# Halved GpSimd instructions, spread weight pieces and opening loads by head, in a fused masked attention and expert layer

## The chip, the cores and the metric

One core of a Trainium2 chip. The metric is the device time of one execution in microseconds (us). Engines: TensorE (PE; PEld is its weight load), VectorE (DVE), ScalarE (ACT), GpSimd (POOL) and SyncE (SP), which issues the DMAs.

## What is computed

```
# q, k, v: (8, 8, 576, 64) f32;  tau = 0.02
scores = q @ k^T / 8
scores = where(scores >= max(scores) - tau, scores, -1e9)      # per row
attn   = exp(scores - max);  attn = attn / (sum(attn) + 1e-9)
x      = (attn @ v), heads joined                              # 4608 x 512
h      = x @ w_in                                              # w_in 512 x 2048, float64
g      = max(h, 0) + alpha * min(h, 0)
out    = g @ w_out                                             # w_out 2048 x 512, float64; out f32
```

## The kernel before

The attention works on 32 pairs of heads, each cut into nine units (a block of 128 query rows of one head, and one unit for the rests of both). The main loop (L832) runs over cycles, one unit each, from cycle -3 to the 288 units and 9 more. In a cycle each engine gets the steps of several units at different depths: scores on TensorE (L403, two cycles ahead, into one of two PSUM buffers), the row maximum on VectorE (L418), the exponential and the threshold on ScalarE (L426, L431), the mask and row sum on VectorE (L438, for the cycle's own unit), transposes (L447), their copies out (L499 to L507), products with v (L550), and for a pair that has ended the reciprocal, the scaling and the store to DRAM (L566 to L604; L597 and L603 are GpSimd's). Up to unit 52 the row maxima go two by two in odd cycles.

Most products are computed with operands split into a rounded part and a rest (two fp32r numbers). For the keys and queries of the pairs after the first, ScalarE rounds (L336, L353) and GpSimd makes the rest (L340, L365); SP moves halves to the other partitions. Pair 0 is prepared in `prep_first` with the rests on VectorE (L327, L330). The pairs 0 to 3 are "whole": their attention weights and v are not split.

The expert layer starts when x of a batch of four pairs is there (`RDY`, cycle 49 for the first). Its first weights are 14 pieces (seven of w_in, seven of w_out, `F1`), float64 words which class `Split64` turns into two fp32r numbers. A piece has a load (SP, L115) and steps that `decode_at` puts into cycles after its start c: at c two ScalarE instructions (L125, L126), at c+1 to c+4 one VectorE instruction each (L129, L132, L137, L142), at c+4 ScalarE's rounding (L146), at c+5 two GpSimd instructions (L150, L151), at c+6 GpSimd's join (L154). The starts are -3, 0, 3, ... 15 for the input pieces and 16, 19, ... 34 for the output pieces. Raw words lie in the slot of a later weight; those of the last output piece in one of two buffers that the loads of k, q and v of the pairs use too. The temporaries come from a pool of four (`spool`, closed at cycle 41) and, after it, from the 11 places (`GB`) of the expert layer's `g` tiles.

Order is written out by hand: instructions stand on each engine in the order in which the cycles emit them, and each engine works its queue in that order. The planner `Mlp` fits first-layer and second-layer products of the expert layer into a cycle by a budget of TensorE time (`room`), and holds back the first layer while 11 `g` tiles live. After the last pair the rest of the expert layer runs alone.

The opening (L819 to L831): SP issues four loads of pair 0's keys, four of its queries, tau, the first weight piece, pair 1's keys and queries, alpha; VectorE's first instruction is tau's negative (L824), then come the splits of `prep_first`.

Of the kernel before, what the change touches and what calls it, by code (L numbers as in the profile page):

```python
# [52 lines left out]
XO = 1  # L53
L2O = 3
# [6 lines left out]
DEC0, DEC = -3, 3  # L61
DECO0, DECO = 16, 3
# [4 lines left out]
def f(ap):  # L67
    return ap.bitcast(F32)


@with_exitstack
def tile_masked_attention_moe(
# [31 lines left out]
    class Split64:  # L104


        def __init__(self, pool, raw, temp_pool, temp, eng, src, a, name):
# [9 lines left out]
        def size(self):  # L117
# [4 lines left out]
            if pool is mem:  # L122
                pool, tag, bufs = (mem.mp1, "g", GB) if mem.mp1 else (spool, "wt", 4)
            self.t = pool.tile([P, DM], I32, tag=tag, name=f"wt{self.name}", bufs=bufs)
            nc.scalar.activation(f(self.t), f(self.high), AF.Abs)  # L125
            nc.scalar.activation(f(self.low), self.low.bitcast(U32), AF.Copy, scale=2.0**-52)  # L126

# [15 lines left out]

        def round(self, hi):
            self.hi = hi
            nc.scalar.activation(hi, f(self.t), AF.Copy)  # L146

        def rest(self):
            low, t = f(self.low), f(self.t)
            self.eng[1].tensor_tensor(low, low, f(self.high), op=ALU.mult)  # L150
            self.eng[2].tensor_tensor(t, t, f(self.hi), op=ALU.subtract)  # L151

        def join(self, lo):
            nc.gpsimd.tensor_tensor(lo, f(self.t), f(self.low), op=ALU.add)  # L154
# [86 lines left out]
    mem = SimpleNamespace(mp1=None)  # L241
# [33 lines left out]
    class Pair:  # L275
# [9 lines left out]
        def load(self, what):  # L285
# [11 lines left out]
            if pi == 0:  # L297

                r = ap1.tile([P, KW if what == "k" else 2 * S], F32, tag="vst" if what == "k" else "p", name=f"{what}r{pi}", bufs=2)
                for j in range(2):  # L300
                    n = w if j else S
                    for half in range(2):
                        nc.sync.dma_start(r[half * D : (half + 1) * D, j * S : j * S + n], src[j * D : (j + 1) * D, :n])
                if what == "k":
                    self.kr = r
                else:
                    self.qr = r[:, : 2 * S].rearrange("p (a b) -> p a b", a=2)
# [8 lines left out]
            else:  # L316
                self.qr = r

# [19 lines left out]
        def prep_kl(self):  # L338
            self.kl = ap1.tile([P, KW], F32R, tag="kl", name=f"kl{self.pi}", bufs=2)
            nc.gpsimd.tensor_tensor(self.kl[:, S:], self.kr, f(self.kh[:, S:]), op=ALU.subtract)  # L340
# [19 lines left out]
        def prep_ql(self):  # L360
            self.qt = ap1.tile([P, S], F32R, tag="qt", name=f"qt{self.pi}", bufs=1)
            if QLV and self.pi >= QLV:
                nc.vector.scalar_tensor_tensor(self.qt, self.qr, 0.125, f(self.qst[:, 0, :S]), op0=ALU.mult, op1=ALU.subtract)
                return
# [674 lines left out]
```

## Time and profile before

| | us |
|---|---|
| median of three runs | 1379.86 |
| the runs | 1378.5 to 1380.6 |
| the profiled execution's own time | 1380.41 |
| its span, first to last instruction | 1378.6 |

In the profile, busy times are the time in which an engine had an instruction, waits inside the instruction included; PE stands for matmuls, whose ends are modelled. L12 is line 12 of the kernel before. The granted TensorE clock is given as a share of full speed.

### The profile page before, as it was taken

How to read it: one execution, taken by the hardware profiler on the slowest of the kernel's cores; microseconds unless marked ns; L12 is line 12 of the kernel's file. 1: busy time of each engine (PE TensorE's matmuls, PEld its weight loads, DVE VectorE, ACT ScalarE, POOL GpSimd, SP SyncE). 2: the span in 40 equal slices, each digit the busy share in tenths (PEclk: the TensorE clock that was granted, in tenths of full speed). 3: DMA queues.
4: the chain of work that ended last, by engine and by line, in shares of the span. 5: the costliest groups of instructions: out<-in, count | busy, mean ns of one | idle time of the engine just before them, and what ended most of it. 6: DMA issues, size and time to landing. Idle time of an engine off the chain costs nothing.

```text
span 1378.6 us, 23959 instructions
## 1 busy us (share of the span) xinstructions
PE 1332.7 (97%) x8116; PEld 1180.2 (86%) x8116; DVE 994.5 (72%) x1970; ACT 842.5 (61%) x1915; POOL 814.9 (59%) x891
## 2 busy tenths in 40 slices
PE   5888899999999999999999999999999999999998
PEld 4556789999999999999999998898888888888887
DVE  6999888888888888889888883883655644333332
ACT  6878888888888888888888873542323321211210
POOL 3776566666666575766666654884757554443431
PEclk9999999999999999999999999999999999999999
DMA  8644643644643644445445413345455452343222
GB/s 252 173 138 112 164 110 109 175 124 112 172 135 114 167 126 128 141 133 142 132 129 150 120 55 110 117 144 169 156 181 187 134 184 92 102 152 113 92 77 77
DMA packets 115178, 186.05 MB, mean 135 GB/s; under 512 B 18320, under 2 KB 49328, under 8 KB 115056
## 3 DMA queue, kind: packets, MB, share of 16 engines
q1 hardware_dynamic: 115056, 184.52, 45.2%
q8 instruction: 65, 1.06, 0.3%
q14 instruction: 57, 0.47, 0.1%
HBM read 104.41 MB, written 37.90 MB: 103 GB/s over the span
## 4 chain that ended last, share of the span: by engine, by line
PE 85%; DVE 6%; ACT 4%; issue 1%; DMA 1%; POOL 1%; SPq 0%; POOLq 0%; DVEq 0%; ACTq 0%
PE accj L232 19%; PE phj L196 18%; PE av L550 11%; PE s L403 11%; PE acca L232 9%; PE pha L196 9%; PE t L447 7%; DVE p L438 2%; DVE nmx L418 1%; PE tk L463 1%; DMA wri<-in_moe_w_in_dram 1%; ACT xb L563 1%; ACT xa L561 1%; ACT xh L182 1%; ACT p L426 0%
## 5 line engine op out<-in xcount | busy, mean ns | idle before, releaser
L418 DVE TENSOR_REDUCE nmx<-s 128x1 f32<-128x576 f32 x288 | 217.2, 754 | 73.2 <-PE s L403 70.1
L223 ACT ACTIVATE gj<-ptj 128x512 fp32r<-128x512 f32 (+1 forms) x109 | 62.9, 577 | 338.1 <-DVE ptj L215 338.1
L226 POOL TENSOR_TENSOR gj<-ptj,gj 128x512 fp32r<-128x512 f32 (+1 forms) x109 | 129.2, 1186 | 237.2 <-ACT gj L223 236.5
L232 PE MATMUL accj<-wo,gj 128*128 128x512 f32 x1140 | 262.4, 390 | 0.6 <-POOL gj L226 0.6
L232 PEld LDWEIGHTS accj<-wo,gj 128*128 128x128 f32 x1140 | 213.9, 188 | 45.1 <-POOL gj L226 1.0
L196 PE MATMUL phj<-xhj,wi 128*128 128x512 f32 (+1 forms) x816 | 232.8, 367 | 0.0
L438 DVE SCALAR_TENSOR_TENSOR p<-s,thr,p 128x576 f32<-128x576 f32 x256 | 206.8, 808 | 1.6 <-ACT thr L431 1.2
L426 ACT ACTIVATE p<-s,nmx 128x576 f32<-128x576 f32 x256 | 190.1, 742 | 10.2 <-DVE nmx L418 9.9
L232 PE MATMUL acca<-wo,ga 128*128 128x512 f32 x588 | 186.1, 423 | 1.6 <-POOL ga L226 0.8
L403 PE MATMUL s<-kh,qst 128*128 128x288 f32 x640 | 142.5, 313 | 38.3 <-DVE p L438 22.1
L196 PEld LDWEIGHTS phj<-xhj,wi 128*128 128x128 f32 x816 | 147.6, 188 | 25.2
L214 DVE TENSOR_SCALAR ptj<-phj,alpha_sb 128x512 f32<-128x512 f32 (+1 forms) x109 | 74.2, 681 | 124.4 <-PE phj L196 120.4
L196 PE MATMUL pha<-xh,wi 128*128 128x256 f32 x784 | 156.9, 284 | 0.2 <-ACT pra L209 0.2
L447 PE MATMUL t<-ident,p 128*128 128x128 f32 x1024 | 154.8, 274 | 0.0
L403 PEld LDWEIGHTS s<-kh,qst 128*128 128x128 f32 x640 | 101.6, 193 | 61.2 <-issue 31.2
L196 PE MATMUL phj<-xlj,wi 128*128 128x512 f32 (+1 forms) x408 | 150.0, 368 | 1.1 <-POOL xlj L810 0.9
L962 DVE TENSOR_TENSOR obj<-accj,pinj 128x512 f32<-128x512 f32 x72 | 49.8, 692 | 138.5 <-PE accj L232 127.7
L403 PE MATMUL s<-kl,qst 128*128 128x288 f32 x640 | 133.7, 299 | 0.0
L196 PEld LDWEIGHTS pha<-xh,wi 128*128 128x128 f32 x784 | 128.1, 190 | 4.4 <-ACT pra L209 1.5
L447 PEld LDWEIGHTS t<-ident,p 128*128 128x128 f32 x1024 | 126.6, 141 | 0.1
L232 PEld LDWEIGHTS acca<-wo,ga 128*128 128x128 f32 x588 | 102.1, 192 | 13.7 <-POOL ga L226 1.2
L219 POOL TENSOR_TENSOR pta<-pta,pra 128x256 f32<-128x256 f32 x94 | 69.4, 739 | 73.9 <-ACT pra L209 71.3
(123 smaller groups left out, 2865.5 us busy)
## 6 DMA issues: line engine op xcount, KB each, us to landing
pinj<-part SPq DMA_DIRECT2D x72, 256.0 KB
kr<-in_k_dram SPq DMA_DIRECT2D x31, 320.0 KB
rb<-rvd SPq DMA_DIRECT2D x64, 144.0 KB
xs<-xa SPq DMA_DIRECT2D x32, 288.0 KB
part<-obj SPq DMA_DIRECT2D x36, 256.0 KB
out_dram<-obj SPq DMA_DIRECT2D x36, 256.0 KB
vr<-in_v_dram SPq DMA_DIRECT2D x28, 320.0 KB
qr<-in_q_dram SPq DMA_DIRECT2D x31, 288.0 KB
```

The costliest lines, as they stand in the source:

```text
L196: nc.tensor.matmul(ph[:, :n], w[:, c, :], xx[:, c, :n], start=(c == 0 and ti == 0), stop=(c == NCC - 1 and ti == 2),)
L214: nc.vector.tensor_scalar(t[:, :n], ph[:, :n], 0.0, alpha_sb[:, fc : fc + 1], op0=ALU.min, op1=ALU.mult)
L219: nc.gpsimd.tensor_tensor(t[:, :n], t[:, :n], r[:, :n], op=ALU.add)
L223: nc.scalar.activation(g[:, 0, :n], t[:, :n], AF.Copy)
L226: nc.gpsimd.tensor_tensor(g[:, 1, :n], t[:, :n], f(g[:, 0, :n]), op=ALU.subtract)
L232: nc.tensor.matmul(acc[:m, :], gg[:, g, o : o + m], w, start=(first and ti == 0), stop=(last and ti == 2))
L403: nc.tensor.matmul(ps[:, h, :288], w, kk[:, a + h * 288 : a + (h + 1) * 288], start=(ki == 0 and i == 0), stop=(ki == 1 and i == n - 1),)
L418: nc.vector.tensor_reduce(self.nmx[:, j : j + 1], self.S[u][0][:, :, :288], axis=AX.XY, op=ALU.max, negate=True)
L426: nc.scalar.activation(pj, ps[:, :, :288], AF.Exp, bias=nmx[:, j : j + 1], scale=1.0)
L438: nc.vector.scalar_tensor_tensor(pj, ps[:, :, :288], thr[:, j : j + 1], pj, op0=ALU.is_ge, op1=ALU.mult, accum_out=self.sm[:, c : c + 1])
L447: nc.tensor.transpose(tb[:, c, :], pt[:, j, j * D + c * P : j * D + (c + 1) * P], ident)
L550: nc.tensor.matmul(pa[:m, :n], w, x, start=(part == 0 and c == 0), stop=(part == z.parts[-1] and c == NKC))
```

## The change

Three things are done. GpSimd's two-tensor instructions of the 14 pieces, of the key and query rests of pairs 1 to 4, and of the scaling of pairs 0 to 3 are each issued as two instructions over half of the columns. The starts of the 14 pieces become -1, 2, 5, 9, 13, 17, 21 (input) and 25, 29, 34, 41, 44, 48, 52 (output); the pieces from cycle 41 on take their temporaries from the `g` places, so the count of living `g` tiles is replaced by a ring in which both stand in order. The loads of pair 0 are issued head by head (keys, then queries), and tau's negative stands behind the splits on VectorE.

```diff
+ROOM = GB - 1
-DEC0, DEC = -3, 3
-DECO0, DECO = 16, 3
+DECC = (-1, 2, 5, 9, 13, 17, 21, 25, 29, 34, 41, 44, 48, 52)
...
+def halves(eng, out, a, b, op):
+
+    h = out.shape[1] // 2
+    for c in (slice(0, h), slice(h, None)):
+        eng.tensor_tensor(out[:, c], a[:, c], b[:, c], op=op)
...
                 pool, tag, bufs = (mem.mp1, "g", GB) if mem.mp1 else (spool, "wt", 4)
+                self.place = None
+                if mem.mp1:
+                    self.place = [False]
+                    mem.ring.append(self.place)
...
+        def turns(self, eng, out, a, b, op):
+            if self.split:
+                halves(eng, out, a, b, op)
+            else:
+                eng.tensor_tensor(out, a, b, op=op)
...
         def rest(self):
             low, t = f(self.low), f(self.t)
-            self.eng[1].tensor_tensor(low, low, f(self.high), op=ALU.mult)
-            self.eng[2].tensor_tensor(t, t, f(self.hi), op=ALU.subtract)
+            self.turns(self.eng[1], low, low, f(self.high), ALU.mult)
+            self.turns(self.eng[2], t, t, f(self.hi), ALU.subtract)
 
         def join(self, lo):
-            nc.gpsimd.tensor_tensor(lo, f(self.t), f(self.low), op=ALU.add)
+            self.turns(nc.gpsimd, lo, f(self.t), f(self.low), ALU.add)
+            if self.place:
+                self.place[0] = True
...
+        def load_first(self):
+            self.kr = ap1.tile([P, KW], F32, tag="vst", name=f"kr{self.pi}", bufs=2)
+            qr = ap1.tile([P, 2 * S], F32, tag="p", name=f"qr{self.pi}", bufs=2)
+            self.qr = qr.rearrange("p (a b) -> p a b", a=2)
+            for j in range(2):
+                for r, src, w in ((self.kr, k, S + j * D), (qr, q, S)):
+                    for half in range(2):
+                        nc.sync.dma_start(
+                            r[half * D : (half + 1) * D, j * S : j * S + w], src[0, 0][j * D : (j + 1) * D, :w]
+                        )
...
         def prep_kl(self):
             self.kl = ap1.tile([P, KW], F32R, tag="kl", name=f"kl{self.pi}", bufs=2)
+            if self.pi <= WHOLE:
+                halves(nc.gpsimd, self.kl[:, S:], self.kr, f(self.kh[:, S:]), ALU.subtract)
+                return
...
+            if self.pi <= WHOLE:
+                halves(nc.gpsimd, self.qt, self.qr, f(self.qst[:, 0, :S]), ALU.subtract)
+                return
             nc.gpsimd.tensor_tensor(self.qt, self.qr, f(self.qst[:, 0, :S]), op=ALU.subtract)
...
         def fin_mul(self):
+            if self.whole:
+                halves(nc.gpsimd, self.x, self.x, self.rb, ALU.mult)
+                return
...
         def fin_out(self):
-            nc.gpsimd.tensor_tensor(self.x, self.x, self.rb, op=ALU.add)
+            if self.whole:
+                halves(nc.gpsimd, self.x, self.x, self.rb, ALU.add)
+            else:
+                nc.gpsimd.tensor_tensor(self.x, self.x, self.rb, op=ALU.add)
...
-            self.live += 1
+            st["place", fi] = [False]
+            mem.ring.append(st["place", fi])
...
             if o + P >= n:
-                self.live -= 1
+                st["place", fj][0] = True
...
-            if self.l1 and i >= self.gap and self.live < GB:
+            if self.l1 and i >= self.gap and all(p[0] for p in mem.ring[:-ROOM]):
...
-        c = DEC0 + DEC * n_ if n_ < F1 else DECO0 + DECO * (n_ - F1)
+        c = DECC[n_]
         load = max(-3, c - LD) if io == "i" else c - 3
...
         p.load("k")
-        p.load("q")
         nc.sync.dma_start(tau_sb, tau.partition_broadcast(P))
-        nc.vector.tensor_scalar(ntau_sb, tau_sb, -1.0, None, op0=ALU.mult)
         pieces[0][0].load()
...
         p.prep_first(0)
         p.prep_first(1)
+        nc.vector.tensor_scalar(ntau_sb, tau_sb, -1.0, None, op0=ALU.mult)
         p.load("v")
```

## Rows read from the trace of the kernel before

**Rows 1.** The page: its head, and PE's busy share in 40 equal slices of the span, in tenths.

```profile
span 1378.6 us, 23959 instructions
PE   5888899999999999999999999999999999999998
```

**Rows 2.** Busy time by stretch (us from the span's start): the stretch, its length, then for each engine busy us and number of instructions, granted clock, share of the DMA engines, GB/s. Pairs 0 to 3, pairs 4 to 6, pair 5 alone, and two pairs later on, each counted from the first row maximum of a pair to that of the next.

```profile
12.90:114.30 101.40, 86.21 (x454) 59.18 (x455) 96.49 (x176) 83.44 (x191) 66.91 (x56) 0.97 0.58 171
114.30:187.50 73.20, 63.53 (x435) 55.30 (x434) 66.80 (x146) 61.61 (x147) 45.82 (x50) 0.98 0.52 139
139.00:162.90 23.90, 18.09 (x129) 17.11 (x128) 20.96 (x46) 20.56 (x49) 11.44 (x11) 0.93 0.57 146
214.60:239.80 25.20, 25.20 (x184) 23.71 (x182) 21.98 (x49) 21.09 (x51) 14.60 (x19) 1.00 0.46 127
239.80:265.10 25.30, 25.30 (x179) 23.66 (x177) 21.81 (x49) 21.98 (x52) 15.18 (x17) 1.00 0.55 153
```

**Rows 3.** The same view for L418 alone, VectorE's row maximum, one for each unit: the stretch, its length, busy us and number. Pair 0 alone and pairs 0 to 3.

```profile
12.90:34.40 21.50, 6.76 (x9) 0.92 0.89 280
...
12.90:114.30 101.40, 27.04 (x36) 0.97 0.58 171
```

**Rows 4.** Groups of VectorE's instructions by line and shape, from 0 to 210 us, the four lines of the weight pieces (wti: input pieces, wto: output pieces): number, busy us, mean ns of one, idle time before them.

```profile
L137 DVE SCALAR_TENSOR_TENSOR wti<-wri,wti 128x512 int32<-128x512 int32 x7 | 8.5, 1221 | 0.0
L132 DVE TENSOR_SCALAR wto<-wto 128x512 int32<-128x512 int32 x7 | 8.4, 1197 | 0.0
L129 DVE TENSOR_SCALAR wto<-wto 128x512 f32<-128x512 f32 x7 | 7.2, 1035 | 0.0
...
L132 DVE TENSOR_SCALAR wti<-wti 128x512 int32<-128x512 int32 x7 | 5.0, 710 | 0.0
...
L137 DVE SCALAR_TENSOR_TENSOR wto<-wro,wto 128x512 int32<-128x512 int32 x7 | 4.9, 694 | 0.0
L142 DVE TENSOR_SCALAR wro<-wto 128x512 int32<-128x512 int32 x7 | 4.6, 652 | 0.0
...
L142 DVE TENSOR_SCALAR wri<-wti 128x512 int32<-128x512 int32 x7 | 3.4, 486 | 0.0
...
L129 DVE TENSOR_SCALAR wti<-wti 128x512 f32<-128x512 f32 x7 | 2.9, 419 | 0.0
```

**Rows 5.** The timeline around 23 us: start, us, engine, line, operation.

```profile
22.64 1.43 POOL L365 TENSOR_TENSOR qt<-qr,qst 128x576 fp32r<-128x576 f32 x1 [1.47 <-ACT qr L358]
...
22.77 1.84 DVE L137 SCALAR_TENSOR_TENSOR wti<-wri,wti 128x512 int32<-128x512 int32 x1
...
24.01 1.74 POOL L154 TENSOR_TENSOR wi<-wti,wri 128x512 fp32r<-128x512 f32 x1
```

**Rows 6.** Groups of GpSimd's instructions by line and shape over the whole span: number, busy us, mean ns of one, idle time before them and what ended it.

```profile
L226 POOL TENSOR_TENSOR gj<-ptj,gj 128x512 fp32r<-128x512 f32 x81 | 105.4, 1302 | 219.0 <-ACT gj L223 219.0
...
L226 POOL TENSOR_TENSOR ga<-pta,ga 128x256 fp32r<-128x256 f32 x98 | 72.3, 738 | 12.8 <-ACT ga L223 5.3
...
L154 POOL TENSOR_TENSOR wo<-wto,wro 128x512 fp32r<-128x512 f32 x16 | 22.8, 1428 | 1.5 <-DVE wto L151 1.2
L154 POOL TENSOR_TENSOR wi<-wti,wri 128x512 fp32r<-128x512 f32 x16 | 22.3, 1394 | 1.8 <-DVE wti L151 1.2
```

**Rows 7.** The timeline of the opening: start, us, engine, line, operation, idle time before it and what ended it. SPq rows are issues of DMAs, merged (x4).

```profile
0.74 2.48 SPq L303 DMA_DIRECT2D kr<-in_k_dram  x4
...
3.27 2.51 SPq L303 DMA_DIRECT2D qr<-in_q_dram  x4
4.44 0.68 ACT L326 ACTIVATE kh<-kr 128x576 fp32r<-128x576 f32 x1 [2.21 <-DMA kr<-in_k_dram]
...
6.99 0.68 ACT L329 ACTIVATE qst<-qr 128x576 fp32r<-128x576 f32 x1 [1.87 <-DMA qr<-in_q_dram]
...
8.21 0.68 ACT L329 ACTIVATE qst<-qr 128x576 fp32r<-128x576 f32 x1
...
8.90 5.74 SPq L115 DMA_DIRECT2D wri<-in_moe_w_in_dram  x5
9.30 0.15 DVE L824 TENSOR_SCALAR ntau_sb<-tau_sb 128x1 f32<-128x1 f32 x1 [9.30 <-DMA tau_sb<-in_tau_dram]
9.41 0.76 DVE L327 TENSOR_TENSOR kl<-kr,kh 128x576 fp32r<-128x576 f32 x1
...
11.01 0.85 PE L403 MATMUL s<-kh,qst 128*128 128x288 f32 x2 [11.01 <-DVE qst L330]
11.23 0.68 ACT L125 ACTIVATE wti<-wri 128x512 f32<-128x512 f32 x1 [2.34 <-DMA wri<-in_moe_w_in_dram]
...
12.97 0.75 DVE L418 TENSOR_REDUCE nmx<-s 128x1 f32<-128x576 f32 x1
...
14.81 0.74 ACT L426 ACTIVATE p<-s,nmx 128x576 f32<-128x576 f32 x1
```

**Rows 8.** Groups of ScalarE's instructions from 0 to 210 us, the three lines of a piece (one of each pair of groups): number, busy us, mean ns of one, idle time before them.

```profile
L126 ACT ACTIVATE wri<-wri 128x512 f32<-128x512 uint32 x7 | 4.7, 673 | 0.0
...
L125 ACT ACTIVATE wti<-wri 128x512 f32<-128x512 f32 x7 | 4.7, 670 | 2.3 <-DMA wri<-in_moe_w_in_dram 2.3
...
L146 ACT ACTIVATE wi<-wti 128x512 fp32r<-128x512 f32 x7 | 4.4, 622 | 0.0
```

More of the change, by code (lines that the diff above doesn't have):

```diff
@@ L104, in tile_masked_attention_moe, with __init__ @@
     class Split64:
-        def __init__(self, pool, raw, temp_pool, temp, eng, src, a, name):
+        def __init__(self, pool, raw, temp_pool, temp, eng, src, a, name, split=False):
+            self.split = split
             self.pool, self.raw_tag, self.temp_pool, self.temp_tag = pool, raw, temp_pool, temp
@@ L126, in size @@
             nc.scalar.activation(f(self.low), self.low.bitcast(U32), AF.Copy, scale=2.0**-52)
+        place = None
         def clamp(self):
@@ L240, in tile_masked_attention_moe @@
     spool = sp.enter_context(tc.tile_pool(name="spool", bufs=1, side="right"))
-    mem = SimpleNamespace(mp1=None)
+    mem = SimpleNamespace(mp1=None, ring=[])
     at, ps = ExitStack(), ExitStack()
@@ L297, in load @@
             if pi == 0:
[L299 to L307, printed above, removed]
+                self.load_first()
                 return
@@ L660, in __init__ @@
             self.acc = None
-            self.live = 0
             self.gap = 0
@@ L757, in tile_masked_attention_moe @@
     for fc in fcs1:
-        pieces.append((Split64(wp1, (f"wo{fc}", 1), mem, ("g", GB), ENG1[fc % 2], *src_i(fc)), fc, "i"))
+        pieces.append((Split64(wp1, (f"wo{fc}", 1), mem, ("g", GB), ENG1[fc % 2], *src_i(fc), split=True), fc, "i"))
     for fc in fcs1:
         stage = (wp1, (f"wo{fc + 1}", 1)) if fc + 1 < F1 else (ap1, ("raw", 2))
-        pieces.append((Split64(stage[0], stage[1], mem, ("g", GB), ENG1[fc % 2], *src_o(fc)), fc, "o"))
+        pieces.append((Split64(stage[0], stage[1], mem, ("g", GB), ENG1[fc % 2], *src_o(fc), split=True), fc, "o"))
     def decode_at(c, pool, w, fc, io, load):
```

## The prediction

> **What bounds the kernel now.** I read the page first, then busy times by stretch, then the timeline of the opening, then VectorE's groups. By the page [rows 1] TensorE is busy nearly everywhere except in the first slices, so what this change can win lies at the front. The stretches [rows 2] say where. In 239.8 to 265.1, an ordinary pair of the middle, PE is busy 25.30 of 25.30 us with 179 matmuls. In 12.9 to 114.3, the pairs 0 to 3 (36 row maxima [rows 3]), 454 matmuls take 101.4 us; VectorE is busy 96.49 us of it (95%), ScalarE 83.44 (82%), GpSimd 66.91 (66%). There VectorE sets the pace. In 114.3 to 187.5, the pairs 4 to 6, VectorE stands at 91%, and in pair 5 alone (139 to 162.9, no weight piece in it) at 88% beside ScalarE's 86%. Microseconds saved before about 200 us reach the end whole: what follows is TensorE's work, and its amount does not change.
>
> Much of VectorE's busy time is no work. Each weight piece takes four VectorE instructions, and the same instruction differs with what GpSimd does [rows 4]: L129 takes 419 ns on the input pieces and 1035 ns on the output pieces, L137 1221 and 694. One instance is plain [rows 5]: GpSimd's L365 starts at 22.64 and lasts 1.43 us, L137 starts at 22.77 and takes 1.84 us, so it did its 0.69 us of work only after L365, and GpSimd's next instruction, L154, takes 1.74 us instead of its mean 1.39 to 1.43 [rows 6], having waited in turn. The two engines exclude each other for an instruction at a time.
>
> **The change part by part.**
>
> *Price of a piece on VectorE.* The eight groups of [rows 4] sum to 44.9 us for 14 pieces. Unhindered, three instructions at 0.419 (L129's quick group, same shape) and one at 0.694 make 1.95 us a piece, 27.3 in all; the other 17.6 us are waiting, 1.26 us a piece.
>
> *Halves.* GpSimd's instructions for the pieces, for the key and query rests of pairs 1 to 4 and for the end of pairs 0 to 3 become two each. 256 columns take 738 ns and 512 take 1302 [rows 6]: a half is 0.57 of a whole, and a split costs 2 x 738 - 1302 = 174 ns. VectorE then waits out a half instead of a whole: 17.6 us become 17.6 x 0.57 = 10.0 us if collisions stay as frequent. GpSimd pays 58 x 0.174 = 10 us spread over some 160 us; at 66% busy it has that room. If the cover were gone, the price would be those 10 us.
>
> *Spreading.* By the code, before, 12.75 pieces have their VectorE steps in cycles up to 34, which is the stretch to 114.3; after, 9 (starts -1 to 29). So 3.75 pieces leave pairs 0 to 3 and fall to pairs 4 to 6 (starts 34 to 52). Pairs 0 to 3 lose on VectorE 3.75 x 1.95 = 7.3 us of work, and waiting falls from 12.75 x 1.26 = 16.1 to 9 x 1.26 x 0.57 = 6.5: 96.5 - 7.3 - 9.6 = 79.6 us. ScalarE loses 3.75 x (0.67 + 0.67 + 0.62) = 7.4 us [rows 8], leaving 76.0. At VectorE's present 95% the stretch would be 83.8 us; but ScalarE has nowhere in [rows 2] been above 87% (21.98 of 25.3), and at 87% it needs 87.4. I take 87.0, close to ScalarE's end: **-14.4 us**, bounds -9 (a share of only 86% of VectorE, below pair 5's) to -17.6.
>
> Pairs 4 to 6 gain VectorE work 7.3 us; their waiting goes from 1.25 x 1.26 = 1.6 to 5 x 1.26 x 0.7 = 4.4 us (0.7, not 0.57, since pairs from 5 on keep whole key and query rests and the ends of pairs 4 and 5 stay whole): 66.8 + 10.1 = 76.9. ScalarE has 61.6 + 7.4 = 69.0. At 95% VectorE needs 80.9, ScalarE at 87% needs 79.3. I take 80.2: **+7.0 us**, bounds +3.7 (no idle VectorE at all) and +10.
>
> *Opening.* Now the eight loads of pair 0 go keys first, then queries; each lands about 3 us after its issue: the last of the first head's queries is issued at 3.90 (second of four from 3.27) and ScalarE takes it at 6.99 [rows 7]. VectorE's first instruction is tau's negative, which waits for tau until 9.30; the key rest queued behind it had its input since 5.12. After: queries of head 0 take the third and fourth issue slots, 0.63 us apart, 2.00 and 2.63, and land near 5.8; L329 ends near 6.5, VectorE's key and query rests of head 0 near 7.3, the first scores start at 7.4 instead of 11.01. Head 1's queries land as before (8.21 for L329), so VectorE's last split ends near 9.7, then tau's negative (landed by 9.3: 0.15 us), and the first row maximum comes near 9.9 instead of 12.97. ScalarE then has the first exponential, the first piece (moved from cycle -3 to -1, its data there at 11.23) and the second exponential in a row, which gives some back. **-2.7 us**, bounds -1.9 (second exponential near 12.9 instead of 14.81) and -3.1.
>
> *At nothing.* Loads of later pieces move with their starts on SP's queue: three instead of five at cycle -3, which sends what follows earlier by up to 2 x 0.6 us; nothing waits for those loads, which come 8 to 12 cycles ahead for input pieces. The last output piece holds one of two raw buffers from cycle 49 to 58 instead of 31 to 40, so pair 7's queries, not pair 5's, get the late load: moved, not removed. The ring's new rule counts the four late pieces among 11 places; they are done by cycle 58, before the second group needs them. The pieces from cycle 41 on use the pool opened there, whose space pair 3 leaves at cycle 40: 0 to 2 us, taken as 0.
>
> *Sum*: -14.4 + 7.0 - 2.7 = -10.1 us. The profiled execution took 1380.4 (span 1378.6), 0.5 above the median 1379.9: I forecast **1370** for the median. A measurement here tells 0.2% (2.8 us) from no change.
>
> **The rivals.**
>
> *The waits don't shorten.* If GpSimd passes from half to half without letting VectorE in, waiting stays 1.26 us a piece. Pairs 0 to 3 then have 96.5 - 7.3 - 4.8 = 84.4, at 95% 88.8 us: -12.6; pairs 4 to 6 66.8 + 7.3 + 4.7 = 78.8, at 95% 83: +9.8; opening -2.7: -5.5, **1374.4**. For it: GpSimd's instructions start before the one ahead has ended (L154 at 24.01, L365 until 24.07). Against it: VectorE's L137 ended at 24.61 with 0.69 us of work, so it came in between just these two [rows 5]. The Trainium skill (GPSIMD Engine Reference, section Instruction dispatch) says that a core starts the next instruction as soon as it has done its own share of the last, nothing holding it back; read strictly this gives the rival's 1374.4. By that rule two halves would lock like one; the trace shows a gap at least between different instructions.
>
> *Slower.* Another bound stands right behind VectorE in pairs 1 to 3: the loop from scores over maximum, exponential and mask through two score buffers. If it holds them at 25.2 us each, the length of 214.6 to 239.8, the stretch with pair 0's 21.5 [rows 3] is 21.5 + 3 x 25.2 = 97.1 (-4.3), pairs 4 to 6 pay +9.8, the opening gives 2.7: +2.8, **1382.7**. It decides once pairs 1 to 3 don't fall below 25.2. For it: pair 5, without pieces, ran VectorE at only 88%. Against it: that pair still took only 23.9 us, with more VectorE work than a whole pair has without pieces.
>
> *More than forecast.* ScalarE lets pairs 0 to 3 run at VectorE's 95%, and pairs 4 to 6 absorb the pieces in idle time: -17.6 + 3.7 - 2.7, **1363**.
>
> **How the numbers follow.** Forecast (1366 to 1374) 0.57; more 0.13; waits that don't shorten 0.17; slower 0.09; gains and losses that cancel 0.04. Range 1361 to 1377: it takes in the first three cases. Faster by over 0.2% 0.82, same 0.10, slower 0.08.
>
> **What would show it.** The first row maximum near 9.9 us; unit 36's row maximum (now 114.3) near 97 and unit 63's (now 187.5) near 177; pair 5 longer than now; VectorE's groups of [rows 4] near 37 us in all instead of 44.9, no instance waiting over 0.9 us before cycle 36; GpSimd halves near 0.74 us. I am wrong if the groups' sum stays above 42 (the waits don't shorten), if pairs 1 to 3 stay above 25 us, or if what is won by unit 63 is not there at the end.

## The result and the profile after

The kernel became slower: 1387.95 us (median; 1387.57 to 1389.03) against 1379.94 us for the kernel before in the same comparison. The ratio is 1.006, with a 95% interval of 1.0046 to 1.0074. Forecast were 1370.0 us, in a range of 1361 to 1377, and, with 0.82, faster. The profiled execution took 1387.57 us.

Lines below are those of the changed kernel: the load of a piece is L123, its ScalarE steps L137, L138 and L166, its VectorE steps L143, L146, L151 and L156, every halved GpSimd instruction L75, the scores L434, the row maximum L449, the exponential L457, the threshold L462, the mask L469, the products with v L581. Pairs are counted from the first row maximum of one to that of the next, as in [rows 2].

The page's head and PE's 40 slices, which answer to [rows 1]: the span is 7.2 us longer, and the loss shows as 8, 7 and 8 in the fourth to sixth slices (104 to 208 us), which were 8, 8 and 9.

```profile
span 1385.8 us, 24008 instructions
PE   6898789999999999999999999999999999999998
```

Busy time by stretch, as in [rows 2]: pairs 0 to 3, pairs 4 to 6, pair 5 alone, pair 6 alone, pair 8.

```profile
core 0: us, PE busy (x) PEld busy (x) DVE busy (x) ACT busy (x) POOL busy (x), PEclk, DMA share, GB/s
9.70:109.10 99.40, 86.51 (x455) 59.52 (x456) 81.94 (x164) 78.12 (x182) 58.21 (x81) 1.00 0.61 183
109.10:195.80 86.70, 70.51 (x447) 61.33 (x445) 78.24 (x161) 69.91 (x162) 63.52 (x82) 0.90 0.44 120
133.70:165.60 31.90, 22.90 (x124) 21.53 (x125) 29.14 (x57) 24.57 (x56) 21.32 (x25) 0.73 0.50 132
165.60:195.80 30.20, 25.34 (x194) 23.84 (x192) 26.01 (x56) 24.71 (x58) 26.02 (x37) 1.00 0.38 107
220.80:246.00 25.20, 25.20 (x183) 23.72 (x182) 22.00 (x49) 21.07 (x52) 14.59 (x19) 1.00 0.46 127
```

The first line is the case in small: against [rows 2] VectorE lost 14.6 us of busy time (96.49 to 81.94), and the stretch lost 2.0 (101.4 to 99.4). The second is the loss: 86.7 us instead of 73.2, nearly all of it in pairs 5 and 6. By stretch: opening -3.3, pairs 0 to 3 -2.0, pairs 4 to 6 +13.5, pair 7 -2.1, nothing from pair 8 to pair 30 (the last line repeats that of before), end +1.1 (its cause was not looked for): +7.2, the difference of the spans.

The row maxima of pair 0, as in [rows 3]: the stretch took 22.7 us instead of 21.5, so over a third of the opening's gain was gone at unit 9. The DMA share rose from 0.89 to 0.92.

```profile
9.70:32.40 22.70, 6.73 (x9) 1.00 0.92 288
```

VectorE's groups for the pieces, 0 to 230 us, as in [rows 4]:

```profile
L151 DVE SCALAR_TENSOR_TENSOR wto<-wro,wto 128x512 int32<-128x512 int32 x7 | 10.1, 1449 | 0.0
L143 DVE TENSOR_SCALAR wto<-wto 128x512 f32<-128x512 f32 x7 | 5.6, 804 | 1.4 <-ACT wto L137 1.4
L151 DVE SCALAR_TENSOR_TENSOR wti<-wri,wti 128x512 int32<-128x512 int32 x7 | 5.4, 772 | 0.0
L146 DVE TENSOR_SCALAR wto<-wto 128x512 int32<-128x512 int32 x7 | 4.8, 683 | 0.0
L143 DVE TENSOR_SCALAR wti<-wti 128x512 f32<-128x512 f32 x7 | 4.5, 650 | 1.1 <-ACT wti L137 1.1
L146 DVE TENSOR_SCALAR wti<-wti 128x512 int32<-128x512 int32 x7 | 4.4, 623 | 0.0
L156 DVE TENSOR_SCALAR wri<-wti 128x512 int32<-128x512 int32 x7 | 3.5, 494 | 0.0
L156 DVE TENSOR_SCALAR wro<-wto 128x512 int32<-128x512 int32 x7 | 3.2, 463 | 0.0
```

They sum to 41.5 us (before 44.9, forecast near 37). The same four lines in the two stretches part them: 23.8 us for the nine pieces up to 109.1, or 2.64 a piece, and 17.8 us for the five after it, 3.56 a piece. Early the halves shortened the waits, late something lengthened them: L151's output group, slow here with 1449 ns, was quick before with 694.

The timeline around 23 us, answering to [rows 5], and then around 159 us (start, us, engine, line, operation):

```profile
22.82 1.42 POOL L75 TENSOR_TENSOR wti<-wti,wi 128x256 f32<-128x256 f32 x2
23.73 0.79 DVE L146 TENSOR_SCALAR wti<-wti 128x512 int32<-128x512 int32 x1
24.20 1.61 POOL L75 TENSOR_TENSOR wi<-wti,wri 128x256 fp32r<-128x256 f32 x2
25.85 0.68 DVE L151 SCALAR_TENSOR_TENSOR wti<-wri,wti 128x512 int32<-128x512 int32 x1
...
159.24 2.37 POOL L206 TENSOR_TENSOR xl<-xr,xh 128x1024 fp32r<-128x1024 f32 x1
159.32 2.85 DVE L151 SCALAR_TENSOR_TENSOR wto<-wro,wto 128x512 int32<-128x512 int32 x1
```

At 23.73 VectorE meets the second of two halves and loses 0.37 us (0.79 against the quick 0.42); at 159.32 it meets a whole instruction of the expert layer, over 1024 columns, and loses 2.2 of its 2.85 us. The Trainium skill (SBUF — State Buffer, section "SBUF: two separate sides") says that whichever of the two engines starts first holds the shared port pair for its whole instruction; the trace agrees: L151 starts 0.08 us after L206 and ends at 162.17, 0.56 us after L206's end at 161.61, a little under the 0.69 us that it takes unhindered.

GpSimd's halves, as in [rows 6]; and one of ScalarE's groups, which are the same as in [rows 8]:

```profile
L75 POOL TENSOR_TENSOR wi<-wti,wri 128x256 fp32r<-128x256 f32 x14 | 10.9, 800 | 0.1
...
L75 POOL TENSOR_TENSOR wo<-wto,wro 128x256 fp32r<-128x256 f32 x14 | 10.7, 783 | 0.0
```

```profile
L137 ACT ACTIVATE wti<-wri 128x512 f32<-128x512 f32 x7 | 4.7, 665 | 0.0
```

The opening, as in [rows 7]:

```profile
1.99 1.23 SPq L340 DMA_DIRECT2D qr<-in_q_dram  x2
...
5.52 0.68 ACT L354 ACTIVATE qst<-qr 128x576 fp32r<-128x576 f32 x1 [0.63 <-DMA qr<-in_q_dram]
...
8.81 0.75 DVE L355 SCALAR_TENSOR_TENSOR qst<-qr,qst 64x576 fp32r<-64x576 f32 x1 [0.21 <-ACT qst L354]
...
9.60 0.15 DVE L866 TENSOR_SCALAR ntau_sb<-tau_sb 128x1 f32<-128x1 f32 x1
9.67 0.75 DVE L449 TENSOR_REDUCE nmx<-s 128x1 f32<-128x576 f32 x1
...
11.37 0.66 ACT L137 ACTIVATE wti<-wri 128x512 f32<-128x512 f32 x1
...
12.49 0.73 ACT L457 ACTIVATE p<-s,nmx 128x576 f32<-128x576 f32 x1
```

The first row maximum starts at 9.67 us, where 9.9 was forecast, and the second exponential at 12.49 us, where 12.9 was.

### The profile page after: what moved, and what is told of

Read it like the earlier page. It is cut to its first block, busy times and chain, and to the rows that moved or that the text cites. A ratio compares the mean times of both kernels' runs of the same rounds, so it can differ in the third digit from the quotient of the medians.

```text
span 1385.8 us, 24008 instructions
## 1 busy us (share of the span) xinstructions
PE 1336.7 (96%) x8116; PEld 1183.1 (85%) x8116; DVE 990.0 (71%) x1970; ACT 842.7 (61%) x1915; POOL 824.5 (59%) x949
## 4 chain that ended last, share of the span: by engine, by line
PE 83%; ACT 6%; DVE 4%; DMA 2%; POOL 2%; issue 2%; SPq 0%; POOLq 0%; ACTq 0%; DVEq 0%
PE accj L254 18%; PE phj L218 18%; PE av L581 10%; PE acca L254 10%; PE s L434 10%; PE pha L218 9%; PE t L478 7%; DVE p L469 1%; PE tk L494 1%; DVE nmx L449 1%; ACT p L457 1%; DMA qr<-in_q_dram 1%; ACT xa L592 1%; DMA vst<-in_v_dram 1%; DMA kl<-kl 1%
## 5 line engine op out<-in xcount | busy, mean ns | idle before, releaser
L449 DVE TENSOR_REDUCE nmx<-s 128x1 f32<-128x576 f32 x288 | 217.1, 754 | 74.2 <-PE s L434 71.3
L469 DVE SCALAR_TENSOR_TENSOR p<-s,thr,p 128x576 f32<-128x576 f32 x256 | 206.8, 808 | 7.7 <-ACT thr L462 7.7
L457 ACT ACTIVATE p<-s,nmx 128x576 f32<-128x576 f32 x256 | 190.0, 742 | 15.9 <-DVE nmx L449 15.8
L434 PE MATMUL s<-kh,qst 128*128 128x288 f32 x640 | 143.5, 315 | 39.0 <-DVE p L469 23.2
L218 PEld LDWEIGHTS phj<-xhj,wi 128*128 128x128 f32 x816 | 147.6, 188 | 25.2
L434 PEld LDWEIGHTS s<-kh,qst 128*128 128x128 f32 x640 | 102.4, 195 | 63.0 <-issue 35.1
L434 PE MATMUL s<-kl,qst 128*128 128x288 f32 x640 | 134.9, 301 | 0.0
```

Of the source, the lines that this page charges most:

```text
L218: nc.tensor.matmul(ph[:, :n], w[:, c, :], xx[:, c, :n], start=(c == 0 and ti == 0), stop=(c == NCC - 1 and ti == 2),)
L434: nc.tensor.matmul(ps[:, h, :288], w, kk[:, a + h * 288 : a + (h + 1) * 288], start=(ki == 0 and i == 0), stop=(ki == 1 and i == n - 1),)
L449: nc.vector.tensor_reduce(self.nmx[:, j : j + 1], self.S[u][0][:, :, :288], axis=AX.XY, op=ALU.max, negate=True)
L457: nc.scalar.activation(pj, ps[:, :, :288], AF.Exp, bias=nmx[:, j : j + 1], scale=1.0)
L469: nc.vector.scalar_tensor_tensor(pj, ps[:, :, :288], thr[:, j : j + 1], pj, op0=ALU.is_ge, op1=ALU.mult, accum_out=self.sm[:, c : c + 1])
```

## The experiments

Theory: VectorE is the bound up to pair 6, and moved pieces cost and save what they take of it. Rivals: another engine stands right behind it in pairs 0 to 3; and in pairs 5 and 6 the loss comes from a late query load, from TensorE's clock, or from the pieces themselves. The table gives the stretches of each kernel (from its own profile); the experiments that it lists follow.

Two things limit how finely it can be read. A stretch comes from one execution: no_vector_late, no_gpsimd_late and more_scores have the changed kernel's instructions in pairs 0 to 3 and took 98.3 to 99.7 us there, nearly all of the difference in pair 0 (22.1 to 23.1 us) and pair 1 (26.9 to 27.5). And the kernel before had medians from 1378.92 to 1380.30 us in the different comparisons, so that two experiments are better compared by their ratios than by their medians.

| kernel | pairs 0 to 3: us | VectorE busy in them | pairs 4 to 6: us | median us | ratio to before, 95% interval |
|---|---|---|---|---|---|
| before | 101.4 | 96.5 | 73.2 | 1379.94 | |
| after | 99.4 | 81.9 | 86.7 | 1387.95 | 1.0046 to 1.0074 |
| starts_only | 100.7 | 86.4 | 87.2 | 1391.29 | 1.0058 to 1.0110 |
| halves_old_starts | 100.2 | 92.3 | 72.0 | 1376.05 | 0.9959 to 0.9980 |
| opening_only | 101.9 | 96.6 | 73.5 | 1378.82 | 0.9981 to 1.0006 |
| no_vector_early | 96.3 | 62.5 | 85.7 | 1384.92 | 1.0033 to 1.0061 |
| less_av | 99.7 | 82.0 | 85.1 | 1386.39 | 1.0034 to 1.0066 |
| less_av_no_vector | 94.7 | 62.3 | 85.0 | 1382.75 | 1.0010 to 1.0032 |
| round_later | 96.5 | 82.3 | 86.4 | 1386.27 | 1.0034 to 1.0065 |
| spread_scalar | 95.1 | 81.6 | 88.1 | 1386.36 | 1.0029 to 1.0063 |
| gated_loads | 97.7 | 81.3 | 85.8 | 1386.96 | 1.0041 to 1.0081 |
| raw_own | 105.3 | 81.5 | 86.4 | 1391.43 | 1.0066 to 1.0113 |
| no_vector_late | 98.3 | 81.8 | 80.2 | 1381.74 | 1.0011 to 1.0035 |
| no_gpsimd_late | 99.5 | 82.0 | 83.3 | 1384.25 | 1.0024 to 1.0048 |
| halves_more | 97.7 | 81.1 | 85.5 | 1384.48 | 1.0028 to 1.0055 |
| more_scores | 99.7 | 82.4 | 86.9 | 1390.38 | 1.0062 to 1.0095 |
| early_starts | 104.7 | 91.5 | 76.8 | 1382.67 | 1.0018 to 1.0037 |
| dense_gated | 102.8 | 94.0 | 72.0 | 1379.36 | 0.9990 to 1.0014 |
| halves_all_old_starts | 98.1 | 92.2 | 71.4 | 1375.42 | 0.9962 to 0.9984 |
| best_spread | 97.6 | 92.2 | 71.8 | 1374.18 | 0.9944 to 0.9973 |

### Which part did it

**halves_old_starts**: the change, with the starts of before.

```diff
-DECC = (-1, 2, 5, 9, 13, 17, 21, 25, 29, 34, 41, 44, 48, 52)
+DECC = (-3, 0, 3, 6, 9, 12, 15, 16, 19, 22, 25, 28, 31, 34)
```

> The changed kernel with the piece starts of before (-3 to 34), halves and the new opening kept. Theory 1, the late pieces (cycles 41 to 58) make the loss: pairs 5 and 6 take about 24 us each again instead of 31.9 and 30.2, and halves and opening give 5 to 9 us: 1371 to 1375. Theory 2, the halves make the loss (more GpSimd time, and VectorE waits as often): at or above 1380, and VectorE's wait on the four lines of the pieces stays near 17 us.

**starts_only**: the change without halves and with the opening of before.

```diff
 def halves(eng, out, a, b, op):
-    h = out.shape[1] // 2
-    for c in (slice(0, h), slice(h, None)):
-        eng.tensor_tensor(out[:, c], a[:, c], b[:, c], op=op)
+    eng.tensor_tensor(out, a, b, op=op)
...
```

> The changed kernel without halves and with the opening of before: only the piece starts are new. Theory 1: slower than the changed kernel or like it, 1387 to 1393, with pairs 5 and 6 above 30 us. Theory 2: near 1380.

**opening_only**: the kernel before with the new opening (whole instructions, the starts of before).

```diff
-DECC = (-1, 2, 5, 9, 13, 17, 21, 25, 29, 34, 41, 44, 48, 52)
+DECC = (-3, 0, 3, 6, 9, 12, 15, 16, 19, 22, 25, 28, 31, 34)
...
+    eng.tensor_tensor(out, a, b, op=op)
```

> The kernel before with only the new opening (loads head by head, tau's negative behind the splits). If the 3 us at the first row maximum are kept: 1377. If the transfers of pair 1 and of the weights, which are queued on SP until 29 us, set the start of pair 1 anyway, the gain shrinks by unit 9 to under 1 us: 1379 to 1380.

The new starts alone cost 11.5 us, halves and opening together win 4 (5 to 9 were expected), the opening alone is within what can be told. With the starts of before pairs 5 and 6 are back at 22.6 and 24.6 us; with the new ones alone they take 30.4 and 29.8. In starts_only the pieces' four lines sum to 47.0 us on VectorE, against 41.5 in the changed kernel: the halves save 5.5 us there. They did what they were for; the starts made the loss. The opening's gain needs the new starts: with the old ones the first row maximum comes at 12.1 and 12.3 us, since the first piece then stands ahead of it (in opening_only its first VectorE step starts at 11.93).

### Pairs 0 to 3: what stands behind VectorE

**no_vector_early**: the four VectorE steps of the first nine pieces left out.

```diff
+        if not (w.split and c < 34):
             at_cycle(c + 1, w.clamp)
...
```

> The changed kernel without the four VectorE steps of the first nine pieces (starts -1 to 29); their weights are then wrong. It frees about 17.5 us of work and some 7 us of waits on VectorE in pairs 0 to 3 (99.4 us now). If VectorE still sets their pace: they fall to about 80 us. If another bound stands close behind (ScalarE's order, the transfers of pair 1, the score buffers): they stay above 90 us.

```profile
9.80:106.10 96.30, 85.43 (x454) 58.78 (x455) 62.46 (x126) 77.30 (x182) 53.86 (x81) 0.98 0.64 189
```

VectorE at 65% busy, and the stretch is still 96.3 us. TensorE's 85.4 us are those of [rows 2] (86.21) and of the changed kernel (86.51): the one number that did not move.

**less_av**: three of the five products of a set with v left out in pairs 0 to 3, which takes work from TensorE alone. **less_av_no_vector**: this and the edit of no_vector_early together.

```diff
-                for c in cs:
+                for c in [c for c in cs if not self.whole or c in (0, NKC)]:
```

> The changed kernel with two of the five products of a set with v in pairs 0 to 3 (their output is then wrong): TensorE loses about 11 us a pair in none, 5 us in each of pairs 1 to 3. If TensorE sets the pace of pairs 0 to 3 by now (99.4 us): 88 to 93 us. If VectorE or ScalarE does: 96 to 99 us.

> Both left out: TensorE's products as in less_av and VectorE's steps of the first nine pieces as in no_vector_early (where pairs 0 to 3 took 96.3 us). If these two engines are the bounds one behind the other: 80 to 86 us. If ScalarE's order and the transfers hold the rest: above 90 us.

```profile
9.90:109.60 99.70, 71.14 (x376) 49.95 (x376) 82.03 (x164) 77.95 (x182) 58.41 (x81) 0.95 0.61 181
```

15 us less of TensorE changed nothing (99.7), 19 us less of VectorE won 3.1 us, both won 4.7. So neither is the bound alone. The chain of waits from 33 to 82 us says the same; its line sums, in this order: before, after, no_vector_early.

```profile
by line: PE av L550 20.7%; PE s L403 16.6%; DVE p L438 12.2%; DVE nmx L418 9.6%; PE t L447 7.1%; DVE wti L137 6.7%; DVE wto L132 3.1%; DVE rv L568 3.1%; DVE wto L129 2.7%; ACT eo L507 2.1%; DVE wti L132 1.8%; issue 1.6%; ACT tt L507 1.4%; D
```

```profile
by line: DVE p L469 13.1%; ACT p L457 10.5%; DVE nmx L449 8.9%; issue 6.4%; ACT wti L137 4.7%; ACT wri L138 4.6%; DMA qr<-in_q_dram 4.5%; ACT thr L462 4.4%; ACT wi L166 4.2%; PE s L434 4.2%; DVE wti L151 4.2%; PE av L581 3.6%; ACT xa L592 3
```

```profile
by line: PE av L581 37.0%; PE s L434 25.1%; PE t L478 13.4%; DVE p L469 3.4%; issue 3.0%; ACT p L457 2.8%; ACT wi L166 2.1%; PE tk L494 1.6%; ACT qst L381 1.4%; ACT xa L592 1.4%; ACT qr L386 1.4%; ACT thr L462 1.4%; ACT kh L361 1.3%; ACT wr
```

Of these 49 us before, TensorE and VectorE hold 22.8 and 22.0. After, ScalarE holds 22.5, VectorE 16.3, TensorE 4.8. Without VectorE's piece work TensorE holds 38.1, and without that and the products (less_av_no_vector) ScalarE 26.6. Take one away and the next is there within some 3 us.

**round_later**: ScalarE's rounding, and GpSimd's steps after it, one cycle later for the first nine pieces. In the changed kernel ScalarE's queue has a bunch between two exponentials; the timeline of ScalarE:

```profile
37.64 0.29 ACT L462 ACTIVATE thr<-nmx,ntau_sb 128x1 f32<-128x1 f32 x1
37.95 0.43 ACT L592 ACTIVATE xa<-av 64x322 f32<-64x322 f32 x1
38.41 0.68 ACT L381 ACTIVATE qst<-qr 128x576 fp32r<-128x576 f32 x1
39.12 0.69 ACT L386 ACTIVATE qr<-qr 128x576 f32<-128x576 f32 x1
39.71 0.61 ACT L166 ACTIVATE wi<-wti 128x512 fp32r<-128x512 f32 x1
40.23 0.66 ACT L137 ACTIVATE wti<-wri 128x512 f32<-128x512 f32 x1
40.80 0.67 ACT L138 ACTIVATE wri<-wri 128x512 f32<-128x512 uint32 x1
41.37 0.57 ACT L538 COPY e<-t 128x512 f32<-128x512 f32 x1
41.83 0.75 ACT L457 ACTIVATE p<-s,nmx 128x576 f32<-128x576 f32 x1
```

With starts four cycles apart, one piece's rounding (start + 4) stands in the same cycle as the next one's two first steps.

```diff
-        at_cycle(c + 4, lambda: w.round(...))
-        at_cycle(c + 5, w.rest)
+        k = 1 if w.split and c < 34 else 0
+        at_cycle(c + 4 + k, lambda: w.round(...))
+        at_cycle(c + 5 + k, w.rest)
...
```

> The changed kernel with ScalarE's rounding of the first nine pieces, and what follows it, one cycle later, so that it no longer falls into the cycle in which the next piece (four cycles on) starts with two ScalarE instructions. If these three in one cycle are what keeps pairs 1 and 3 at 27.4 and 26.7 us while VectorE idles: each falls by 1 to 3 us, 1383 to 1386. If not: 1387 to 1389.

**spread_scalar**: this, and the second of the two first steps (L138) three cycles later for all 14 pieces.

```diff
+        if w.split:
+            at_cycle(c + 3, w.size_low)
...
```

> The run round_later (1386.3; pairs 0 to 3 in 96.5 us) with the second of ScalarE's two starting instructions of every piece three cycles later, so that no cycle holds more than one of a piece's ScalarE instructions. If ScalarE's order is what holds pairs 0 to 3 now that VectorE waits less: another 1 to 3 us there, 93.5 to 95.5, and 1383 to 1385. If that was all in the rounding: 1386.

In round_later pairs 0 to 3 fell to 96.5 us with VectorE's work as it was, as much as leaving out all of that work gave. GpSimd's steps moved too, so this run alone does not part ScalarE's order from theirs. spread_scalar moves only an instruction of ScalarE beyond it, and the stretch fell to 95.1 us, as expected (pairs 1 to 3 from 73.7 to 71.7). Here are its pairs 1 to 3, and its chain from 33 to 82 us by line (L585 are the products with v, L438 the scores, L482 and L498 transposes):

```profile
33.20:104.90 71.70, 68.71 (x371) 44.96 (x370) 62.82 (x125) 59.47 (x138) 50.02 (x71) 1.00 0.56 162
```

```profile
by line: PE av L585 47.5%; PE s L438 30.1%; PE t L482 16.0%; PE tk L498 1.8%; DVE nmx L453 1.5%; DVE p L473 1.5%; PE rp L608 0.9%; issue 0.8%; PE tk_t L496 0.2%
```

TensorE holds 47.4 of these 49 us (68.4 of the 71.7 of pairs 1 to 3) and is busy 96% of pairs 1 to 3. So once ScalarE's instructions no longer stand in a bunch, TensorE is the bound, with all of VectorE's work in place. Little of it reached the end: pair 4 took 25.9 us in round_later and 27.3 in spread_scalar instead of 24.6, and spread_scalar's median, 1386.36, missed the 1383 to 1385 expected.

**gated_loads**: the loads of input pieces 2 to 6 held back, by a write of GpSimd into their raw buffers and issue five instead of twelve cycles ahead.

```diff
-LD = 12
+LD = 5
...
+            if self.split and self.name in ("i2", "i3", "i4", "i5", "i6"):
+                nc.gpsimd.memset(self.raw.bitcast(F32)[:, :2], 0.0)
```

> The changed kernel with the loads of input pieces 2 to 6 issued five cycles ahead of their start (a small write by GpSimd holds each back) instead of nearly all before 17 us. If the full transfer queue (pair 1's moves take 8 to 10 us to land there) eats the opening's gain: the moves land in about 3 us, pair 1's first row maximum comes at 30.5 to 31.5 instead of 32.4, and the kernel takes 1386 to 1387. If not: no difference at that unit.

Pair 0 took 21.5 us instead of 22.7, and pair 1's first row maximum came at 31.3. In the changed kernel the chain from 5 to 36 us holds a move of pair 1's key rests (`DMA kl<-kl`) for 7.51 us from 20.92 on, and in gated_loads it holds none. So part of the opening's gain was lost to transfers that share the DMA engines with pair 1's. Pairs 0 to 3 won 1.7 us in all. The median is 1.0 us lower, but the ratio, 1.0061 against the changed kernel's 1.0060, is not: no gain at the end can be told.

### Pairs 4 to 6: why so much

**raw_own**: an own raw buffer for the last output piece, so that no query load waits for it.

```diff
-        stage = (wp1, (f"wo{fc + 1}", 1)) if fc + 1 < F1 else (ap1, ("raw", 2))
+        stage = (wp1, (f"wo{fc + 1}", 1)) if fc + 1 < F1 else (ap1, ("rawo", 1))
```

> The changed kernel with a buffer of its own for the raw words of the last output piece, so that pair 7's queries need not wait for the key rest of pair 7. If that late load (4.6 us in the chain at 168 us) is what stretches pair 6: 1383 to 1385, pair 6 near 26 us. If GpSimd's and VectorE's queues are the reason and the load only hides them: 1387 to 1388.

Pair 7's queries are now issued 7.9 us before pair 6's first row maximum (163.56) instead of 2.7 us after it (168.34), and pairs 5 and 6 stay at 31.9 and 29.8 us (after: 31.9, 30.2): the late load is not the cause. The median lies in neither range, since pair 0 took 26.9: the freed load is issued at 21.05, ahead of moves of pair 1's keys and queries, the last of which is issued at 32.42 instead of 29.00. In SP's order an early load is no gift.

**no_vector_late**: the four VectorE steps of the last four pieces left out. **no_gpsimd_late**: two of their three GpSimd steps left out instead.

```diff
-        at_cycle(c + 1, w.clamp)
...
+        if not (w.split and c > 40):
+            at_cycle(c + 1, w.clamp)
...
```

> The changed kernel without the four VectorE steps of the last four pieces (starts 41, 44, 48, 52); their weights are then wrong. If VectorE's added work and its waits on GpSimd stretch pairs 5 and 6 (31.9 and 30.2 us): both fall to 24 to 26 us, 1375 to 1378. If GpSimd's queue does it: pair 6 stays above 28 us, 1383 or more.

> The changed kernel without the multiply and the subtract on GpSimd (two of three GpSimd steps) of the last four pieces; their weights are then wrong. If GpSimd's queue stretches pairs 5 and 6: 24 to 26 us each, near 1376. If it is VectorE's own added work: pair 5 stays near 29, only VectorE's waits get shorter, 1383 to 1385.

Without the VectorE steps pair 5 falls to 26.8 us and pairs 4 to 6 to 80.2, without the GpSimd steps to 83.3: 6.5 and 3.4 of the 13.5 us. Pair 6 stays at 29.3 and 28.1. no_vector_late lies between its two cases: VectorE's work is a good part of pair 5, but not of pair 6.

**halves_more**: halves also for pairs up to 7 and for the expert layer's first L206.

```diff
-            if self.pi <= WHOLE:
+            if self.pi <= 7:
...
-        nc.gpsimd.tensor_tensor(xl[:, :, :n], xr[:, :, :n], f(xh[:, :, :n]), op=ALU.subtract)
+        (halves if t0 < 512 else whole)(nc.gpsimd, xl[:, :, :n], xr[:, :, :n], f(xh[:, :, :n]), ALU.subtract)
```

> The changed kernel with GpSimd's large instructions of pairs 4 to 7 and of the first two expert groups' input rests in halves too. If VectorE's waits on whole GpSimd instructions stretch pairs 5 and 6 (5.1 us of waits between 140 and 175 us): 1384 to 1386. If the added GpSimd time (0.17 us each) counts more, with GpSimd at 26.0 of 30.2 us in pair 6: 1388 to 1390.

VectorE's busy time in pair 5 falls from 29.2 to 26.7 us, the pair from 31.9 to 30.9. The median falls by 3.5 us (by the ratios 2.6). Pairs 4 to 6 win 1.2 us; of the 1.7 in pairs 0 to 3, 0.7 is in pair 3, where VectorE had met the whole v rest of pair 4 (L414, a wait of 1.03 us at 102.24). The four VectorE steps of the five late pieces now take 13.2 us, 2.64 a piece as early, instead of 17.8: the whole instructions are why late pieces cost more on VectorE. But 4.6 us less of VectorE shortened pairs 4 to 6 by only 1.2, so of the late loss they are a small part.

**more_scores**: the product with the key rests done twice in units 43 to 60. In the changed kernel TensorE ran at 0.50, that is 1.2 GHz, in these two stretches of pairs 5 and 6 (stretch, length, busy times, granted clock):

```profile
137.60:147.80 10.20, 8.20 (x35) 7.83 (x36) 8.48 (x20) 6.81 (x15) 6.61 (x9) 0.50 0.94 237
154.60:161.40 6.80, 5.28 (x24) 5.28 (x25) 6.76 (x12) 5.30 (x13) 6.80 (x7) 0.50 0.21 69
```

```diff
-            for ki, kk in enumerate((self.kh, self.kl)):
+            more = (self.kl,) if 43 <= 9 * self.pi + u <= 60 else ()
+            for ki, kk in enumerate((self.kh, *more, self.kl)):
```

> The changed kernel with TensorE's product of the key rest issued twice in units 43 to 60 (the rest counts double there), 0.4 us more TensorE work a unit. TensorE is granted half its clock from 137.6 to 147.8 and from 154.6 to 161.4 us, after a stretch in which it was busy 2.84 of 6 us. If that clock is a good part of pair 5's 31.9 us: with more to do the clock stays up, pair 5 falls to 27 to 30 us and the kernel takes 1384 to 1387. If the clock only follows the delay: pair 5 stays or grows, 1388 to 1392.

The stretches at half clock in these pairs shrank from 17.0 to 6.8 us in all, and pairs 5 and 6, with the added products in them, still took 31.5 and 30.7 us: the clock did not make the loss. It can be about 1 us of it. Among the kernels whose instructions from pair 5 on are the changed kernel's, pair 5 took 31.8 and 31.9 us at a granted clock of 0.73 (less_av, after), 31.1 and 31.3 at 0.78 (gated_loads, less_av_no_vector), 30.7 at 0.83 (round_later) and 30.8 at 0.89 (no_vector_early). Whether the clock made that difference or followed it is not shown.

### Versions

**early_starts**: the input pieces as in the change, the last four pieces done by cycle 40. **dense_gated**: starts at -1, 1, 3, 6, then as before, with the loads held back.

```diff
-DECC = (-1, 2, 5, 9, 13, 17, 21, 25, 29, 34, 41, 44, 48, 52)
+DECC = (-1, 2, 5, 8, 11, 13, 16, 19, 21, 24, 26, 29, 31, 34)
```

```diff
-DECC = (-1, 2, 5, 9, 13, 17, 21, 25, 29, 34, 41, 44, 48, 52)
+DECC = (-1, 1, 3, 6, 9, 12, 15, 16, 19, 22, 25, 28, 31, 34)
```

> The changed kernel with all 14 starts between -1 and 34 (-1, 2, 5, 8, 11, 13, 16, 19, 21, 24, 26, 29, 31, 34), halves and opening kept. If the late pieces are the loss and the first piece's place at -1 carries the opening's gain: 1372 to 1374, below the run with the starts of before (1376). If the density of pieces up to 34 eats the opening's gain: 1376.

> The changed kernel with starts -1, 1, 3, 6, 9, 12, 15, 16, 19, ... 34 (those of before but for the first three) and the held-back loads of the run gated_loads. If only the late pieces lose and the opening's 3 us can be kept: 1371 to 1374, under the run with the starts of before (1376). If the order of the first pieces matters as in the run early_starts: 1376 to 1382.

early_starts missed both of its ranges, and dense_gated lies in the second of its own. In early_starts pair 3 took 31.6 us with no engine over 24.4 us busy; why was not found. In dense_gated pairs 0 and 1 took 24.3 and 28.7 us and gave the opening's gain back.

**halves_all_old_starts**: halves_more with the starts of before. **best_spread**: that, and L138 two cycles after the start.

```diff
+            at_cycle(c + 2, w.size_low)
...
```

> Halves also in pairs 4 to 7 (as in halves_more), with the starts of before. With no late pieces few instructions of VectorE meet the halved ones of pairs 4 to 7 (2.7 us of waits after 114 us in the kernel before): 1374.5 to 1376, against 1376 without them.

> The run halves_all_old_starts (1375.4) with the second starting instruction of ScalarE two cycles later. VectorE is still at 94% in pairs 1 to 3 there, so ScalarE's order should matter less: 1373.5 to 1375.5; if ScalarE holds it up as in the changed kernel: 1371 to 1373.

best_spread, 1374.18 us, has the lowest median here, 0.9958 of the kernel before, and can't be told from the two kernels that it builds on: two of its four runs were granted the full clock (1.000) and took 1373.29 and 1373.52 us, and the one run each of halves_old_starts and halves_all_old_starts with that clock took 1373.29 and 1373.35. Its two stretches:

```profile
12.30:109.90 97.60, 85.65 (x452) 58.66 (x453) 92.17 (x176) 84.14 (x192) 75.88 (x105) 1.00 0.60 179
109.90:181.70 71.80, 61.60 (x432) 53.66 (x431) 66.61 (x146) 61.48 (x148) 49.19 (x75) 1.00 0.51 141
```

It runs VectorE at 94% and TensorE at 88% in pairs 0 to 3, as long as no_vector_early did within 1.3 us, with all the work in it.

## Why the prediction was wrong

**The step that failed is "Spreading"**: "At VectorE's present 95% the stretch would be 83.8 us; but ScalarE ... at 87% it needs 87.4. I take 87.0". The amounts were right: VectorE's busy time was to fall to 79.6 us and fell to 81.9, ScalarE's to 76.0 and it has 78.1. What was wrong is turning an amount into a time by one engine's share. The third engine's number stood in the same row: TensorE 86.21 us [rows 2]. At 87.0 us it would have had to be busy 99%, in a stretch whose pair 0 alone leaves it idle for 5 us (21.5 us long, 16 busy). With pair 0 at 21.5 us, 65.5 were left for pairs 1 to 3, where TensorE was busy 70.2 us before and 69.3 after the change. I passed over it since there were 454 matmuls where later pairs have some 180 each; but it was work, for when less_av left matmuls out, it fell by 15 us. Measured was -2.0 us instead of -14.4: unit 36's row maximum came at 109.1 us, not near 97. The bounds behind VectorE, as far as the runs part them, are ScalarE's order, which holds the changed kernel at about 99 us (moving its instructions apart took off 2.9 and then 1.4), and right behind it TensorE at about 95 (spread_scalar). ScalarE's order alone, with less work on VectorE and TensorE, holds the stretch at 94.7 (less_av_no_vector, where ScalarE holds the larger part of the chain).

**Pairs 4 to 6** failed by the same step, +13.5 instead of +7.0. VectorE's work was sized well again, 78.2 us against 76.9, and the 95% did not hold: it was 90%. The pieces add to all three engines in pairs whose attention weights are split and where the expert layer begins. The runs give 6.5 us for VectorE's steps, 3.4 for GpSimd's and 1.2 for GpSimd instructions left whole, three sizes that overlap, the first with up to 1 us of clock in it (0.87 granted in pair 5 instead of 0.73). What the rest is, 2.4 us or more, stays open: ScalarE's 9.8 us of piece work there and the ring that makes late pieces and `g` tiles take places in order were not tried apart.

**Halves** were right. At 2.64 us a piece early, the forecast was 1.95 + 1.26 x 0.57 = 2.67. The groups of the pieces' halves lie between 654 and 800 ns with their waits, where 738 was taken. Late pieces came to 3.56 instead of 2.83: a factor of 0.7 was too small for the instructions left whole, the L206 of 1024 columns above all, which was not in the account; halved (halves_more), they leave 2.64.

**The waits don't shorten**, the rival, falls: VectorE comes in between halves. The groups' 47.0 us without halves against 41.5 with them show that two halves do not lock like one. The rule of the Trainium skill beside it (GPSIMD Engine Reference, section Instruction dispatch) is about when a core starts its next instruction and says nothing of the port between two instructions; that two halves would lock like one was the prediction's reading of it.

**Opening**: the first row maximum came 3.3 us earlier where 3.1 was forecast, the second exponential 2.3 (12.49 instead of 14.81), so that the term of -2.7 was right there; but at unit 18 only -0.8 is left. A gain in the first exponential was counted as a gain at the end; it was spent in pairs 0 and 1 on transfers (gated_loads) and on ScalarE's order (round_later). "Microseconds saved before about 200 us reach the end whole" holds from pair 8 on, not from the first microsecond.

**At nothing**: right for the late raw buffer (raw_own). The ring was not tried by itself.

**The rival "slower"**, 1382.7 us with 0.09, was nearest. Pairs 1 to 3 took 76.7 us, 25.6 each, and it said 25.2; that they stay above 25 was one of the prediction's own signs of being wrong, while the groups' sum, 41.5, stayed just under the 42 of the other. Its mechanism is not shown: no loop through two score buffers holds pairs at 25.2, for pair 2 alone took 22.5. That another bound stands right behind VectorE is shown, and pair 5's 88% was the hint that deserved more than 0.09.

## What to carry to other kernels

Before taking work off the engine that is busiest, put every engine's busy time of that stretch, TensorE's too, beside the length that you forecast: no engine's busy time can be longer than the stretch, and three engines at 95, 85 and 82% give a few per cent at best (here 95.1 of 101.4 us, and only after ScalarE's order was changed too). Work moved into a stretch where a new phase starts can cost more than it takes of the busiest engine: here 13.5 us for 11.4 more of VectorE's busy time, while the stretch that it left won 2.0. Take a change of three parts apart first: here two of them won 4 us, and the third cost 11.5.

## What the runs showed of the hardware

Stretches at half the TensorE clock (1.2 GHz) stood at different places in different kernels; the profiled execution of halves_all_old_starts has none. One of them in pair 7, a pair bound by TensorE (the kernel before, granted clock 0.57 from 196 to 200 us), goes with 27.1 us for that pair, where opening_only, without one there, takes 25.7: 1.4 us, about the whole difference between those two profiled spans (1378.6 and 1377.1). The executions of one kernel differ in the same way: in the comparisons of the experiments, those of the kernel before with a mean granted clock of 1.000 took 1376.2 to 1377.9 us, and those with 0.994 or 0.995 took 1378.9 to 1382.7. Part of a difference of 1 to 3 us between two medians can therefore be the clock. In pairs 5 and 6, bound by waits, 10 us less at half clock (17.0 against 6.8 in more_scores) did not shorten them, though there TensorE had more to do.
